# Epsilon as a third triple of the statistics aggregation, a mean scaled in ScalarE's accumulator, and a newly searched instruction order, in a one-core MLP-mixer block

## The chip, the cores and the metric

The kernel runs on one core of one Trainium2 chip. The metric is the device time of one execution in microseconds. Besides the time, every run lists its *span*, from the first to the last instruction of the core.

I use one more length, the *real stretch*: from the start of the first real matmul (tile 1's row matmuls) to the start of the last residual add, both read from the chain of waits. It separates most of the start-up from the rest. One part of the start-up stays inside it: the four row matmuls at its head. They took 1.02 us in most traces, but 1.05 in a_unmean, 1.08 in a_unfold and 1.10 in a_start, where the first of them was slow. Differences of 0.1 us or less are therefore not read as an effect of the change. In the expectations that are quoted below, the same length is given to the modelled end of TensorE's last matmul, which is 0.03 to 0.05 us earlier.

## The reference, cut to what matters

```python
B, S, D, F = 1, 2048, 512, 1792          # bfloat16 throughout

def reference(x, w1, w2, w3, w4):
    h = _gelu(_layernorm(x, axis=-1) @ w1)               # eps 1e-5 in the variance
    # the four quarters of h's channels are shifted by +1, -1, +2, -2 tokens
    hs = jnp.concatenate([g0, g1, g2, g3], axis=-1) @ w2
    x1 = x + hs
    h2 = _gelu(_layernorm(x1, axis=-1) @ w3) @ w4
    return x1 + h2
```

There are 2048 tokens in 16 tiles of 128. Each tile is normalised twice (as x and as x1), so there are 32 statistics; below they are numbered q = 0 to 15 for x and 16 to 31 for x1.

## The kernel before: the parts that matter

The program is a graph of operations. TensorE's order is written down in a script. The other engines' orders come from a list scheduler with priorities, and tables say which engine does what. Everything was tuned by search.

```python
STAT_ACT = (1, 4, 6, 7, 12, 14, 19, ...)     # statistics on ScalarE; the others on VectorE
VPE = {0: "pool", 2: "pool", 4: "pool", ...} # "+ eps" on GpSimd; the others on VectorE
SCRIPT = """
warm:11 ty:1 ty:0 up1:1 ty:2 up1:0 th:1 up1:2 mix:0 ty:3 mix:1 ty:4 up1:3-4 ty:5 mix:2 up1:5 mix:3 ty:16-17
mix:4 up2:0 up1:6 down:0-1 ...
"""
```

Here `warm:11` is 11 matmuls on zeros that are meant to bring the clock up, `ty:n` is the TensorE transpose of a normalised tile n, `up1` and `up2` are the matmuls with w1 and w3, `mix` those with w2 and `down` those with w4. Tile 1 is the first one: its `up1:1` is done in row form, on the rows less their mean, and the standard deviation is put in later by the GELU's scale.

The statistics of one tile, in the two variants:

```python
if q in STAT_ACT:                                    # ScalarE: sum and sum of squares
    act : sum   activation(junk, src, Copy,   accum_out=sums[:, q, 0:1])       # layer 1
    act : ssq   activation(junk, src, Square, accum_out=sums[:, q, 1:2])
    dve : mean  mv[:, q, 0:1] = sums[:, q, 0:1] * (1 / D)
    dve : msq   mv[:, q, 1:2] = mean * mean - eps
    dve : vpe   vpe[q] = ssq / D - msq
else:                                                # VectorE
    dve : bnst  bn_stats(st6[:, q, :], src)          # 6 numbers: two triples
    dve : bnag  bn_aggr(mv[:, q, :], st6[:, q, :])   # mean, variance
    dve or pool : vpe[q] = variance + eps
pool: rstd      rstd[q] = vpe[q] ** -0.5
...             xn = (x - mean) * rstd               # VectorE, ScalarE or GpSimd, by table
```

This is abridged from the kernel's `ln`. The transpose that follows, by TensorE or by DMA, waits for `xn`.

## Time and profile before

| | before |
|---|---|
| time, median of 4 runs | 135.94 us (135.6 to 136.02) |
| span of the profiled run | 134.5 us |
| TensorE busy | 131.4 us, 98% of the span |
| VectorE, ScalarE, GpSimd busy | 54.5, 57.1, 26.9 us |
| first real matmul, real stretch | 6.15 us, 126.50 us |

The engines' busy time, from the page's first part (engine, busy us, share of the span, number of instructions):

```profile
PE 131.4 (98%) x791; PEld 71.8 (53%) x791; DVE 54.5 (41%) x162; ACT 57.1 (42%) x91; POOL 26.9 (20%) x63
```

The chain that ended last, in order of time (start us, us, what):

```profile
0.64 4.51 PE o_ps L700 x11
5.15 0.24 PE y_ps L503 x4
...
5.41 0.61 ACT xnT L511
6.01 0.14 issue
6.15 1.02 PE y_ps L541 x4
...
11.36 0.22 PE y_ps L503 x4
...
132.65 0.29 DVE o_sb L684
```

The chain is TensorE itself but for one piece. L700 are the warm-ups, L503 the transposes, L541 tile 1's row matmuls. Between them TensorE waits while ScalarE evacuates tile 1's transpose (L511, 0.61 us). After 6.15 us no piece of the chain belongs to another engine until the last residual add.

Of the two small instructions that the change removes, the first is this group on the page (source line, engine, operation, shapes, count | busy us, mean ns of one | idle us before it and what ended it). The second, L398, is seen in VectorE's timeline of tile 1's chain (start us, us, what):

```profile
L426 POOL TENSOR_SCALAR vpe<-mv 128x1 f32<-128x1 f32 x10 | 2.3, 233 | 18.0 <-DVE mv L421 17.8
```

```profile
3.32 0.14 DVE L398 TENSOR_SCALAR mv<-sums 128x1 f32<-128x1 f32 x1
3.44 0.18 DVE L421 BATCH_NORM_AGGREGATE mv<-st 128x2 f32<-128x6 f32 x1
3.54 0.32 DVE L454 TENSOR_SCALAR xn_buf<-x_sb,mv 128x512 bf16<-128x512 bf16 x1
```

The separate epsilon is 233 ns on GpSimd (10 tiles) or about 150 ns on VectorE (8 tiles). The separate mean (L398) is 0.14 us. Tile 1's row is ready at 3.54 + 0.32 = 3.86 us, more than 1 us before TensorE takes it.

### The profile page before, as it was taken

To read this page: it belongs to the slowest core of one execution; us is meant where nothing else is said; L and a number is where in the kernel's file an instruction comes from. 1 tells how busy PE (TensorE), PEld (TensorE's weight loads), DVE (VectorE), ACT (ScalarE), POOL (GpSimd) and SP (SyncE) were. 2 spreads that over 40 slices of the span, in tenths; PEclk is the share of its full clock that TensorE was granted. 3 is DMA by queue.
4 is the path that set the end of the run, shared out by engine and by line. 5 is a ranking of instruction groups with operands and counts; after the bars stand their busy time and mean duration, and the time that the engine had idled before them with its cause. 6 is when DMAs were issued, how large, how long until landed. Compare 5 with 4: busy or idle time off the path is not lost.

```text
span 134.5 us, 2035 instructions
## 1 busy us (share of the span) xinstructions
PE 131.4 (98%) x791; PEld 71.8 (53%) x791; DVE 54.5 (41%) x162; ACT 57.1 (42%) x91; POOL 26.9 (20%) x63
## 2 busy tenths in 40 slices
PE   8899999999999999999999999999999999999994
PEld 3388688644566444444444458744444444444463
DVE  2879899689387510171006235052200002232222
ACT  6589625394648866656660003640066530000000
POOL 2645546968044300021002001010000000000000
DMA  6999995644555311003000311103110001111112
GB/s 200 324 385 400 353 255 106 173 81 91 107 120 119 78 39 39 0 0 78 0 0 5 78 39 39 39 0 78 44 39 0 0 0 39 39 44 39 39 42 77
DMA packets 21290, 12.19 MB, mean 91 GB/s; under 512 B 13856, under 2 KB 20768, under 8 KB 21280
## 3 DMA queue, kind: packets, MB, share of 16 engines
q1 hardware_dynamic: 20560, 11.67, 30.9%
q10 hardware_dynamic: 720, 0.39, 1.0%
q8 instruction: 6, 0.10, 0.3%
q14 instruction: 4, 0.03, 0.1%
HBM read 6.82 MB, written 2.10 MB: 66 GB/s over the span
## 4 chain that ended last, share of the span: by engine, by line
PE 98%; ACT 0%; DVE 0%; issue 0%; POOLq 0%
PE y_ps L607 46%; PE o_ps L676 36%; PE o_ps L647 10%; PE o_ps L700 3%; PE y_ps L503 1%; PE y_ps L541 1%; ACT xnT L511 0%; DVE o_sb L684 0%; PE o_ps L578 0%; POOLq L839 0%
## 5 line engine op out<-in xcount | busy, mean ns | idle before, releaser
L607 PE MATMUL y_ps<-xnT,w_sb 128*128 128x512 bf16 (+2 forms) x424 | 63.6, 309 | 0.0
L607 PEld LDWEIGHTS y_ps<-xnT,w_sb 128*128 128x128 bf16 x424 | 38.3, 98 | 24.7 <-DVE xnT L511 0.4
L676 PE MATMUL o_ps<-w_sb,h2T 128*128 128x512 bf16 (+2 forms) x252 | 49.1, 355 | 0.0
L622 ACT ACTIVATE h2T<-y_ps 128x1024 bf16<-128x1024 f32 (+1 forms) x29 | 28.6, 993 | 37.7 <-PE y_ps L607 37.7
L676 PEld LDWEIGHTS o_ps<-w_sb,h2T 128*128 128x128 bf16 x252 | 23.6, 98 | 24.9
L684 DVE TENSOR_TENSOR o_sb<-o_ps,x_sb 128x512 bf16<-128x512 f32 (+2 forms) x18 | 11.3, 630 | 39.9 <-PE o_ps L676 39.9
L437 POOL TENSOR_TENSOR rstd<-vpe,neghalf 128x1 f32<-128x1 f32 x32 | 18.0, 568 | 43.5 <-DVE vpe L405 17.3
L647 PE MATMUL o_ps<-w_sb,hT 128*128 128x512 bf16 x64 | 15.8, 379 | 0.0
L419 DVE BATCH_NORM_STATS2 st<-x_sb 128x6 f32<-128x512 bf16 x18 | 12.2, 688 | 3.4 <-DMA x_sb<-in_x_dram 3.2
L458 DVE TENSOR_SCALAR xn_buf<-x_sb,mv,rstd 128x512 bf16<-128x512 bf16 x20 | 9.5, 476 | 7.3 <-POOL rstd L437 4.1
L658 DVE TENSOR_TENSOR x_sb<-o_ps,x_sb 128x512 bf16<-128x512 f32 x8 | 5.5, 685 | 16.6 <-PE o_ps L647 16.3
L394 ACT ACTIVATE junk<-x_sb 128x512 bf16<-128x512 bf16 x14 | 8.7, 623 | 3.7 <-DVE x_sb L654 3.5
L622 ACT ACTIVATE hT<-y_ps 128x512 bf16<-128x512 f32 (+1 forms) x10 | 8.1, 808 | 3.4 <-PE y_ps L607 3.3
L647 PEld LDWEIGHTS o_ps<-w_sb,hT 128*128 128x128 bf16 x64 | 6.1, 98 | 5.7
L654 DVE SCALAR_TENSOR_TENSOR x_sb<-o_ps,x_sb 128x512 bf16<-128x512 f32 x8 | 5.5, 689 | 7.7 <-PE o_ps L647 7.7
L426 POOL TENSOR_SCALAR vpe<-mv 128x1 f32<-128x1 f32 x10 | 2.3, 233 | 18.0 <-DVE mv L421 17.8
L467 ACT ACTIVATE xn_buf<-x_sb,nmr,rstd 128x512 bf16<-128x512 bf16 x5 | 4.0, 810 | 2.6 <-DVE nmr L463 2.5
L700 PE MATMUL o_ps<-zeros 128*128 128x512 bf16 x11 | 4.5, 595 | 0.6 <-POOLq L839 0.6
L470 POOL TENSOR_SCALAR xn_buf<-x_sb,rstd,nmr 128x512 bf16<-128x512 bf16 x6 | 4.6, 774 | 0.1
L389 ACT ACTIVATE junk<-x_sb 128x512 bf16<-128x512 bf16 x6 | 3.8, 625 | 2.0 <-DMA x_sb<-in_x_dram 2.0
L700 PEld LDWEIGHTS o_ps<-zeros 128*128 128x128 bf16 x11 | 1.5, 143 | 3.1 <-issue 2.5
L421 DVE BATCH_NORM_AGGREGATE mv<-st 128x2 f32<-128x6 f32 x18 | 3.0, 173 | 0.2
(33 smaller groups left out, 30.6 us busy)
## 6 DMA issues: line engine op xcount, KB each, us to landing
out_dram<-o_sb SPq DMA_DIRECT2D x15, 128.0 KB, 1.7
w_sb<-in_w_dram SPq DMA_DIRECT2D x2, 896.0 KB, 9.0
w_sb<-in_w_dram SPq DMA_DIRECT2D x1, 1792.0 KB, 14.2
w_sb<-in_w_dram SPq DMA_DIRECT2D x4, 256.0 KB, 4.8
x_sb<-in_x_dram SPq DMA_DIRECT2D x3, 256.0 KB, 4.6
x_sb<-in_x_dram SPq DMA_DIRECT2D x2, 384.0 KB, 6.1
xnT<-xn_buf SPq DMA_TRANSPOSE x24, 2.5
x_sb<-in_x_dram SPq DMA_DIRECT2D x2, 128.0 KB, 5.9
```

The lines of the kernel that those rows point to most:

```text
L394: (lambda d: (lambda e: e.activation(d, src, ACT_F.Square, accum_out=sums[:, q, 1:2])))(junk[:, b, :]),
L419: pg.add("dve", f"bnst{q}", lambda e: e.bn_stats(st6[:, q, :], src), reads=rs, writes=[(("st6", q), 0)], dur=605)
L437: lambda e: e.tensor_tensor(col(rstd), col(vpe), neghalf[:], ALU.pow),
L458: lambda e: e.tensor_scalar(dst, src, mv[:, q, 0:1], rstd[:, q : q + 1], ALU.subtract, ALU.mult),
L607: ins = e.matmul(y_ps[:, p, W * i : W * (i + 1)], wsb[:, dc, P * fc : P * (fc + 1)], src[:, dc, P * t0 : P * t0 + W], start=(dc == 0), sto ...
L622: (lambda d, s: (lambda e: e.activation(d, s, ACT_F.Gelu_apprx_tanh)))(dst, ysrc),
L647: ins = e.matmul(dst, hT[:, j, c0 : c0 + P], w2_sb[:, j, :], start=(j == 0), stop=(j == DC - 1))
L654: f = lambda e: e.scalar_tensor_tensor(x1_sb[:, t, :], dst, 1.0, x_sb[:, t, :], ALU.mult, ALU.add, accum_out=sums[:, NT + t, 0:1])
L658: f = lambda e: e.tensor_tensor(x1_sb[:, t, :], dst, x_sb[:, t, :], ALU.add)
L676: ins = e.matmul(dst, h2T[:, fc, P * t : P * (t + 1)], w4_sb[:, fc, cs], start=(fc == 0), stop=(fc == FC - 1))
L684: (lambda d, c: (lambda e: e.tensor_tensor(o_sb[:, oi, c], d, x1_sb[:, t, c], ALU.add)))(dst, cs),
L700: ins = e.matmul(o_ps[:, b, :], zeros[:, 0:P], zeros[:], start=True, stop=True)
```

## The change

Its intent has three parts.

1. Epsilon goes into the aggregation. The kernel takes what `bn_stats` leaves as two triples (count, mean, count times variance). A third triple (0, 0, D times eps), written once, is meant to make `bn_aggr` return variance + eps, so that "+ eps" goes away.
2. ScalarE's `Copy` scales by 1/D, so its accumulator is the mean, and the VectorE multiply goes away in layer 1.
3. All tables, the load order and TensorE's script are searched anew, with a refined model of loads and of the cold clock. The hand-found priorities are dropped.

```diff
-        st6 = sb("st6", [P, 2 * NT, 6], F32)
+        st9 = sb("st9", [P, 2 * NT, 9], F32)
+            pg.add("pool", "trip0", lambda e: e.memset(st9[:, :, 6:8], 0.0), ...)
+            pg.add("pool", "trip1", lambda e: e.memset(st9[:, :, 8:9], D * LN_EPS), ...)
 ...
-    e.activation(d, src, ACT_F.Copy, accum_out=sums[:, q, 0:1])
+    e.activation(d, src, ACT_F.Copy, scale=1.0 / D, accum_out=mv[:, q, 0:1])
 ...
-    pg.add("dve", f"bnag{q}", lambda e: e.bn_aggr(mv[:, q, :], st6[:, q, :]), ...)
-    pg.add(VPE.get(q, "dve"), f"vpe{q}",
-           lambda e: e.tensor_scalar(col(vpe), mv[:, q, 1:2], LN_EPS, None, ALU.add), ...)
+    pg.add("dve", f"bnag{q}", lambda e: e.bn_aggr(mv[:, q, :], st9[:, q, :]), ...)
+    var = vpe[:, q : q + 1] if q in STAT_ACT else mv[:, q, 1:2]      # rstd reads it
 ...
-tp16 x0@act x1 w1a w1b x3-4 w2b w2a x5-7 x9-11 w3a w3b x8 w4 tp10 x12-13 x14-15 x2@act
+x0-1 x2 ... w1a ... w1b ... x3 x4-5 w2b w2a ... x7 x8 x6 w3b ... w3a ... x9-10 w4b w4a tp9 x11 x12 x15 x13-14 ...
 ...
-warm:11 ty:1 ty:0 up1:1 ty:2 up1:0 th:1 up1:2 mix:0 ty:3 mix:1 ty:4 up1:3-4 ty:5 mix:2 up1:5 mix:3 ty:16-17 ...
+warm:10 ty:1 ty:0 up1:1 ty:2 up1:0 th:1 up1:2 mix:0 ty:3-4 mix:1 ty:5 up1:3-4 mix:2 ty:16-17 mix:4 up2:0 ...
```

This is cut; the scheduler's model and the other tables (which engine normalises, evacuates, does statistics) change too. TensorE's work stays the same but for one warm-up.

More of the change, by code (lines that the diff above doesn't have):

```diff
@@ L31 @@
     LOOK = {"dve": 300.0, "act": 300.0}
-    DUE = 202650.0
+    DUE = 258005.0
     BEGIN = {"sp": 30.0, "act": 150.0, "pe": 400.0, "dve": 150.0, "pool": 450.0}
     ENTRY = 1900.0
+    COLD, RESTART = 4300.0, 800.0
     LAG = {"load": 150, "tp": 700}
@@ L159, in place @@
         rings = {"sp": [], "act": []}
-        clock = moved = self.total = 0.0
+        fed = {}
+        clock = moved = last = self.total = 0.0
         out = []
@@ L196, in land @@
         def land(op):
-            nonlocal moved
+            nonlocal moved, last
             if op.queue == "tp":
-                at = max(clock + 500.0, op.start + 2450.0) + self.LAG["tp"]
+                at = max(clock + 500.0, op.start + 2450.0, last + 600.0) + self.LAG["tp"]
             elif op.name.startswith("out"):
@@ L204, in land @@
                 moved += op.dur
-                at = clock + 650.0 + min(450.0, 0.25 * moved) + (1200.0 if op.dur > 1400.0 else 0.0) + self.LAG["load"]
+                at = clock + 600.0 + min(600.0, 0.3 * moved) + (600.0 if op.dur > 1400.0 else 0.0) + self.LAG["load"]
+            if op.queue != "tp":
+                last = max(last, at)
+            op.landed = at
             for j in succs[op.idx]:
@@ L230, in place @@
                 tp = op.queue == "tp"
-                free[e] = start + (1300.0 if tp else 460.0)
-                rings[e].append([start + (1400.0 if tp else 1000.0), 600.0 if tp else op.dur, op])
+                free[e] = start + (1300.0 if tp else 500.0)
+                load = op.name.startswith("dma")
+                work = 600.0 if tp else op.dur + (self.RESTART if load and not fed.get(e, True) else 0.0)
+                fed[e] = load
+                rings[e].append([start + (1400.0 if tp else 1000.0), work, op])
                 for j in succs[op.idx]:
@@ L236, in place @@
             else:
-                free[e] = start + op.dur
+                dur = op.dur
+                if e == "pe" and not op.name.startswith("warm"):
+                    dur += min(dur, max(0.0, self.COLD - start))
+                free[e] = start + dur
                 for j in succs[op.idx]:
@@ L240, in place @@
                     hop = self.HOP[e] if o.eng != e else (0.0 if e == "pe" else 120.0)
-                    release(op, o, None if (op.idx, j) in order_only else start + op.dur + hop)
+                    release(op, o, None if (op.idx, j) in order_only else start + dur + hop)
         while (op := finish(1e17)) is not None:
@@ L245, in place @@
         return out
-GROUPS = {1: (1, 1, 1, 1, 1, 1, 2, 4, 2, 2), 2: (2, 4, 4, 4, 2)}
-NORM = {4: "pool", 9: "pool", 11: "pool", 13: "act", 15: "pool", 16: "act", 18: "pool", 20: "pool", 24: "act", 25: "act", 27: "act"}
-EVAC = {2: "dve", 4: "both", 5: "dve", 7: "dve", 8: "dve", 10: "dve", 11: "dve", 16: "dve", 17: "dve", 18: "dve", 19: "dve", 20: "both", 22: "both", 26: "dve", 27: "dve", 28: "both", 29: "both", 31: "dve"}
-SQRT = ()
-STAT_ACT = (1, 4, 6, 7, 12, 14, 19, 21, 23, 24, 25, 27, 29, 31)
@@ L252 @@
-HALF = ()
+GROUPS = {1: (1, 1, 1, 1, 2, 2, 4, 1, 2, 1), 2: (2, 4, 2, 4, 4)}
+NORM = {3: "act", 8: "act", 9: "pool", 10: "pool", 11: "pool", 12: "pool", 14: "act", 15: "pool", 16: "act", 18: "act", 19: "act", 21: "act", 23: "act", 24: "act", 25: "pool", 27: "pool", 28: "act", 29: "pool", 30: "pool", 31: "act"}
+EVAC = {2: "dve", 5: "both", 6: "dve", 8: "dve", 9: "dve", 10: "both", 12: "dve", 14: "dve", 15: "dve", 16: "both", 17: "both", 18: "dve", 19: "both", 21: "dve", 26: "both", 30: "both", 31: "dve"}
@@ L253 @@
+STAT_ACT = (1, 8, 9, 10, 12, 13, 14, 15, 18, 22, 24, 25, 27, 29, 31)
 TAIL = (256, 128, 128)
-VPE = {0: "pool", 2: "pool", 4: "pool", 5: "pool", 6: "pool", 8: "pool", 9: "pool", 14: "pool", 16: "pool", 17: "pool", 19: "pool", 20: "pool", 22: "pool", 24: "pool", 25: "pool", 26: "pool", 31: "pool"}
-NMR = {2: "pool", 3: "pool", 4: "pool", 6: "pool", 7: "pool", 9: "pool", 10: "pool", 11: "pool", 12: "pool", 14: "pool", 18: "pool", 21: "pool", 23: "pool", 25: "pool", 26: "pool", 28: "pool", 29: "pool", 30: "pool", 31: "pool"}
+NMR = {0: "pool", 2: "pool", 3: "pool", 4: "pool", 6: "pool", 7: "pool", 9: "pool", 11: "pool", 12: "pool", 13: "pool", 18: "pool", 19: "pool", 20: "pool", 21: "pool", 22: "pool", 28: "pool", 29: "pool"}
@@ L256 @@
 NAT = (1,)
 SPLIT = ()
-HEV = {1: "dve", 6: "dve"}
-BIAS = {"bnag1": 67, "bnag10": -301, "bnst1": -2084, "bnst10": 1027.66, "bnst14": -605, "bnst15": -1013, "bnst16": -53, "bnst22": -213.193, "bnst7": 1154, "mean1": -1316.81, "mean4": -714.654, "mean5": 1358, "mean8": -649, "msq19": 938, "msq21": -357, "msq3": -971, "msq5": -137.984, "nmr13": -638.801, "nmr15": -1354.5, "nmr16": -514, "nmr19": -721, "norm0": 1112.57, "rstd0": -1069, "rstd10": 709, "rstd16": 1002, "rstd24": 487, "rstd30": -520, "ssq1": -299, "sum12": 418.607, "sum14": 58, "sum15": 149, "sum18": -577, "tp1": -866, "tp19": 1482.81, "tp22": 632.325, "tp3": 119, "tp9": -705.339, "vpe3": 86, "vpe4": -591, "x1_0": 412.151, "x1_11": 1046, "x1_14": -897, "x1_5": 670, "x1_6": 572.538}
+HEV = {1: "dve", 3: "dve"}
@@ L260 @@
+BIAS = {}
 LOADS = """
-tp16 x0@act x1 w1a w1b x3-4 w2b w2a x5-7 x9-11 w3a w3b x8 w4 tp10 x12-13 x14-15 x2@act
+x0-1 x2 tp17 tp16 w1a tp2 w1b tp5 x3 x4-5 w2b w2a tp16 x7 x8 x6 w3b tp1 w3a tp0 x9-10 w4b w4a tp9 x11 x12
+x15 x13-14 tp4
 """
 SCRIPT = """
-warm:11 ty:1 ty:0 up1:1 ty:2 up1:0 th:1 up1:2 mix:0 ty:3 mix:1 ty:4 up1:3-4 ty:5 mix:2 up1:5 mix:3 ty:16-17
-mix:4 up2:0 up1:6 down:0-1 up1:7 mix:5-6 up1:9 mix:9 mix:8 up1:8 mix:7 mix:15 up2:1 mix:14 mix:13 up2:2
-mix:10 down:3-4 down:8 mix:12 up2:4 mix:11 down:2 down:7 down:5 up2:3 down:6 down:10-11 down:9 down:14
@@ L267 @@
-down:12-13 down:15
+warm:10 ty:1 ty:0 up1:1 ty:2 up1:0 th:1 up1:2 mix:0 ty:3-4 mix:1 ty:5 up1:3-4 mix:2 ty:16-17 mix:4 up2:0
+mix:3 up1:5 down:1 down:0 mix:5 up1:6 mix:6 up1:7 mix:9-10 up1:8 mix:7-8 up2:1 mix:12 mix:11 up1:9 mix:13
+up2:2 mix:15 up2:3 mix:14 down:5 down:9 down:2 down:4 up2:4 down:6 down:8 down:3 down:12 down:7 down:10
+down:13 down:11 down:14-15
 """
@@ L303, in bass_standalone__mixer_s_mlp__prompt_kernel @@
         nmr = sb("nmr", [P, 2 * NT], F32)
-        sdv = sb("sdv", [P, 2 * NT], F32)
         sums = sb("sums", [P, 2 * NT, 2], F32)
-        st6b = sb("st6b", [P, len(HALF) + 1, 2, 6], F32)
         hn = sb("hn", [P, len(NAT) + 1, D], BF16)
@@ L343, in consts @@
                    reads=[(("ident",), 0)], writes=[(("ident",), 1)], dur=300)
+            pg.add("pool", "trip0", lambda e: e.memset(st9[:, :, 6:8], 0.0), writes=[(("trip", 0), 0)], dur=90)
+            pg.add("pool", "trip1", lambda e: e.memset(st9[:, :, 8:9], D * LN_EPS), writes=[(("trip", 1), 0)], dur=80)
             pg.add("pool", "epsc", lambda e: e.memset(eps_c[:], LN_EPS), writes=[(("eps",), 0)], dur=70)
@@ L356, in load @@
                 t0, t1 = int(a), int(b or a) + 1
-                if t0 in HALF:
-                    for hh, e2 in ((0, "sp"), (1, "act")):
-                        cs = slice(hh * D // 2, (hh + 1) * D // 2)
-                        yield pg.add(e2, f"dma_x{t0}_{hh}",
-                                     (lambda c: (lambda e: e.dma_start(x_sb[:, t0, c], xt[:, t0, c])))(cs),
-                                     writes=[(("x", t0, hh), 0)], dur=190.0, queue=e2)
-                else:
-                    yield pg.add(eng, f"dma_x{t0}",
-                                 lambda e: e.dma_start(x_sb[:, t0:t1, :], xt[:, t0:t1, :]),
-                                 writes=[(("x", t, hh), 0) for t in range(t0, t1) for hh in (0, 1)],
-                                 dur=(t1 - t0) * 430.0, queue=eng)
+                yield pg.add(eng, f"dma_x{t0}", lambda e: e.dma_start(x_sb[:, t0:t1, :], xt[:, t0:t1, :]),
+                             writes=[(("x", t), 0) for t in range(t0, t1)], dur=(t1 - t0) * 380.0, queue=eng)
             else:
@@ L375, in load @@
                              writes=[((name[:2], c), 0) for c in range(c0, c1)],
-                             dur=(c1 - c0) * P * src.shape[1] * 2 / (300.0 if src.shape[1] == D else 380.0), queue=eng)
+                             dur=(c1 - c0) * P * src.shape[1] * 2 / (345.0 if src.shape[1] == D else 400.0), queue=eng)
                 yield op
@@ L382, in ln @@
             src = x_sb[:, t, :] if layer == 1 else x1_sb[:, t, :]
-            rs = [(("x", t, 0), 0), (("x", t, 1), 0)] if layer == 1 else [(("x1", t), 0)]
+            rs = [(("x", t), 0)] if layer == 1 else [(("x1", t), 0)]
             col = lambda a: a[:, q : q + 1]
@@ L388, in ln @@
                     pg.add("act", f"sum{q}",
-                           (lambda d: (lambda e: e.activation(d, src, ACT_F.Copy, accum_out=sums[:, q, 0:1])))(
-                               junk[:, b, :]),
-                           reads=rs, writes=[(("sum", q), 0), (("junk", b), v)], dur=610)
+                           (lambda d: (lambda e: e.activation(d, src, ACT_F.Copy, scale=1.0 / D,
+                                                              accum_out=mv[:, q, 0:1])))(junk[:, b, :]),
+                           reads=rs, writes=[(("mv", q), 0), (("junk", b), v)], dur=610)
                 b, v = next_junk()
@@ L396, in ln @@
                        reads=rs, writes=[(("ssq", q), 0), (("junk", b), v)], dur=610)
-                pg.add("dve", f"mean{q}",
-                       lambda e: e.tensor_scalar(mv[:, q, 0:1], sums[:, q, 0:1], 1.0 / D, None, ALU.mult),
-                       reads=[(("sum", q), 0)], writes=[(("mv", q), 0)], dur=75)
+                if layer == 2:
+                    pg.add("dve", f"mean{q}",
+                           lambda e: e.tensor_scalar(mv[:, q, 0:1], sums[:, q, 0:1], 1.0 / D, None, ALU.mult),
+                           reads=[(("sum", q), 0)], writes=[(("mv", q), 0)], dur=75)
                 pg.add("dve", f"msq{q}",
@@ L408, in ln @@
             else:
-                if layer == 1 and t in HALF:
-                    k = HALF.index(t)
-                    for hh in (0, 1):
-                        pg.add("dve", f"bnst{q}_{hh}",
-                               (lambda hh: (lambda e: e.bn_stats(st6b[:, k, hh, :],
-                                                                 src[:, hh * D // 2 : (hh + 1) * D // 2])))(hh),
-                               reads=[rs[hh]], writes=[(("st6", q, hh), 0)], dur=335)
-                    pg.add("dve", f"bnag{q}", lambda e: e.bn_aggr(mv[:, q, :], st6b[:, k, :, :]),
-                           reads=[(("st6", q, 0), 0), (("st6", q, 1), 0)], writes=[(("mv", q), 0)], dur=90)
-                else:
-                    pg.add("dve", f"bnst{q}", lambda e: e.bn_stats(st6[:, q, :], src),
-                           reads=rs, writes=[(("st6", q), 0)], dur=605)
-                    pg.add("dve", f"bnag{q}", lambda e: e.bn_aggr(mv[:, q, :], st6[:, q, :]),
-                           reads=[(("st6", q), 0)], writes=[(("mv", q), 0)], dur=75)
@@ L423, in ln @@
-                if q not in SQRT:
-                    eng = VPE.get(q, "dve")
-                    pg.add(eng, f"vpe{q}",
-                           lambda e: e.tensor_scalar(col(vpe), mv[:, q, 1:2], LN_EPS, None, ALU.add),
-                           reads=[(("mv", q), 0)], writes=[(("vpe", q), 0)], dur=70 if eng == "dve" else 240)
-            if q in SQRT:
-                assert q not in STAT_ACT
-                pg.add("act", f"sqrt{q}",
-                       lambda e: e.activation(col(sdv), mv[:, q, 1:2], ACT_F.Sqrt, bias=eps_c[:], scale=1.0),
-                       reads=[(("mv", q), 0), (("eps",), 0), (("warm",), 0)], writes=[(("sdv", q), 0)], dur=190)
-                pg.add("dve", f"rcp{q}", lambda e: e.reciprocal(col(rstd), col(sdv)),
-                       reads=[(("sdv", q), 0)], writes=[(("rstd", q), 0)], dur=75)
-            else:
-                pg.add("pool", f"rstd{q}",
-                       lambda e: e.tensor_tensor(col(rstd), col(vpe), neghalf[:], ALU.pow),
-                       reads=[(("vpe", q), 0), (("neghalf",), 0)], writes=[(("rstd", q), 0)], dur=470)
+                pg.add("dve", f"bnst{q}", lambda e: e.bn_stats(st9[:, q, 0:6], src),
+                       reads=rs, writes=[(("st", q), 0)], dur=605)
@@ new lines, in ln @@
+                pg.add("dve", f"bnag{q}", lambda e: e.bn_aggr(mv[:, q, :], st9[:, q, :]),
+                       reads=[(("st", q), 0), (("trip", 0), 0), (("trip", 1), 0)],
+                       writes=[(("mv", q), 0), (("vpe", q), 0)], dur=75)
+            var = vpe[:, q : q + 1] if q in STAT_ACT else mv[:, q, 1:2]
+            pg.add("pool", f"rstd{q}",
+                   lambda e: e.tensor_tensor(col(rstd), var, neghalf[:], ALU.pow),
+                   reads=[(("vpe", q), 0), (("neghalf",), 0)], writes=[(("rstd", q), 0)], dur=470)
@@ L658, in mm_mix @@
                 f = lambda e: e.tensor_tensor(x1_sb[:, t, :], dst, x_sb[:, t, :], ALU.add)
-            pg.add("dve", f"x1_{t}", f, reads=[(("o", b), v), (("x", t, 0), 0), (("x", t, 1), 0)], writes=wr, dur=600)
+            pg.add("dve", f"x1_{t}", f, reads=[(("o", b), v), (("x", t), 0)], writes=wr, dur=600)
             ln(2, t)
@@ L706, in warm_pe @@
             next_bank()
-        if SQRT:
-            pg.add("act", "warm_sqrt", lambda e: e.activation(warm[:], eps_c[:], ACT_F.Sqrt),
-                   reads=[(("eps",), 0)], writes=[(("warm",), 0)], dur=1400)
         pg.add("act", "warm_gelu", lambda e: e.activation(warm[:], eps_c[:], ACT_F.Gelu_apprx_tanh),
-               reads=[(("eps",), 0)] + [(("sdv", q), 0) for q in SQRT], writes=[(("warm",), 1)], dur=1400)
+               reads=[(("eps",), 0)], writes=[(("warm",), 1)], dur=1400)
         steps = []
```

## The prediction

> **What bounds the kernel now.** TensorE, almost without a gap. The page gives PE 131.4 us busy of a 134.5 us span (98%), granted clock 1.00. The chain of waits is PE for 98% of the span. In time order: 0.64 us to the first warm-up; 11 warm-ups until 5.15; transposes of tiles 1 and 0; a 0.6 us hole in which ScalarE evacuates tile 1's transpose; the first real matmul at 6.15; then PE pieces without a break to 132.63; then 1.9 us of tail (last residual add 0.29, output DMA).
>
> **What the change removes, adds, moves.**
> - Epsilon in the aggregation: 18 "+eps" instructions go (10 on GpSimd at 233 ns, 8 on VectorE at about 150 ns: about 3.5 us of engine time, and one semaphore hop per tile).
> - Mean scaled in ScalarE's accumulator: the VectorE multiply (0.14 us) goes from the first-layer ScalarE tiles. On tile 1, first on PE, that saves about 0.25 us with its hop.
> - Assignment: ScalarE gets 11 normalisations instead of 5 (0.81 us each) and 8 full-statistics tiles instead of 6 (about 1.6 us each), about +8 us; VectorE loses nine normalisations (about 0.45 us each) and the small ops, about -6 us. Estimate: ACT 57 to 65, DVE 54.5 to 49, POOL about 27.
> - PE work: same tile groups by count (five singles, three pairs, one quad, one row tile; two pairs and three quads in layer 2), the same eight PE transposes, one warm-up fewer. Matmuls 791 to 790.
>
> **How much lies on the critical path.** Almost none of the small-op savings. Tile 1's normalised row is finished near 3.9 us, but PE first takes it at 4.98, when the warm-ups end: that chain has 1 us of slack already. What counts is the dropped eleventh warm-up. By the trace warm-ups 1 to 10 start 0.43 us apart, the eleventh 0.32 after the tenth and the first transpose 0.21 after it: the clock came up during the tenth, as the Trainium skill ("TensorE: Matmul & The Clock Gate", Part 1) describes (cold 426.7 ns, warm 215.7 ns at 512 columns, after a window of about 3.4 us). So the eleventh costs only about 0.21 us. Gain: 0.2 us, if w1 (its second half lands near 5.5 us) doesn't get later behind the merged x0-1 load.
> Loads have slack: w3 lands about 14.8 and is first used at 17.4 (new order: needed 0.86 us earlier, with fewer x tiles ahead); w4 about 20.5, used at 25.2.
>
> **Against it.** After 6.15 a new order can only tie or open gaps. Tightest: tile 4's transpose comes about 1 us earlier, tiles 16/17 likewise (tile 17's row was ready 0.1 us before PE took it), and ScalarE, which also does the GELU, gets busier before 30 us. I expect 0 to 0.8 us of new gaps, mean 0.25.
>
> **Prediction.** 135.9 us, 135.3 to 136.9. Faster by over 2%: 0.01; within 2%: 0.95; slower: 0.04.
>
> **What would show each step.** First transpose near 4.77, first real matmul near 5.9; PE gaps after that under 0.8 us in total, all before 30 us; tail unchanged at 1.9 us; no +eps group; aggregation near 0.18 us as before (0.173); rstd waiting on the aggregation itself; ACT busy up by about 8 us.
>
> **What would make it wrong.** The merged x0-1 load or w1 landing over 0.7 us later; the clock coming up later than PE's first real matmuls; a missed transpose DMA after 35 us, which would open a gap of over 1 us.

## The result, and the profile after

| | before | after |
|---|---|---|
| time, median of 4 runs each | 135.94 us | 136.03 us (135.73 to 136.11) |
| ratio after / before | | 1.0007, 95% interval 0.9984 to 1.003 |
| span of the profiled run | 134.5 us | 134.4 us |
| VectorE, ScalarE, GpSimd busy | 54.5, 57.1, 26.9 us | 49.8, 63.9, 27.5 us |
| first real matmul | 6.15 us | 5.88 us |
| real stretch | 126.50 us | 126.66 us |

A ratio is the mean time of one kernel's fast runs over the mean of the other's in the same rounds, so it isn't quite the ratio of the medians. The first real matmul and the real stretch are of the profiled runs.

The busy times after, from the page's first part. Thirteen matmul records are missing from this trace (777 matmuls for 790 weight loads; a group of four shows as three, for instance), so TensorE's busy time isn't comparable to the last digit:

```profile
PE 130.7 (97%) x777; PEld 71.7 (53%) x790; DVE 49.8 (37%) x141; ACT 63.9 (48%) x106; POOL 27.5 (20%) x62
```

The chain after, in order of time:

```profile
0.64 4.25 PE o_ps L680 x10
4.88 0.24 PE y_ps L483 x4
...
5.14 0.61 ACT xnT L491
5.75 0.14 issue
5.88 1.02 PE y_ps L521 x4
...
10.45 0.86 PE o_ps L627 x4
11.31 0.36 PE y_ps L483 x4
...
132.54 0.29 DVE o_sb L664
```

Two things differ. The warm-ups are one fewer, and the first real matmul starts 6.15 - 5.88 = 0.27 us earlier. And at 11.31 the transpose of tile 5 takes 0.36 instead of 0.22 us of the chain: 0.14 us of it is a hole. The rest of the chain is as gapless as before. The sum is -0.27 + 0.14 = -0.13 us, against 132.54 - 132.65 = -0.11 us measured at the chain's end. That is a third of the spread between runs of one kernel (135.6 to 136.02), so the times can't show it.

The hole is explained by VectorE's timeline together with TensorE's:

```profile
10.04 0.69 DVE L638 TENSOR_TENSOR x_sb<-o_ps,x_sb 128x512 bf16<-128x512 f32 x1
10.80 0.41 DVE L438 TENSOR_SCALAR xn_buf<-x_sb,mv,rstd 128x512 bf16<-128x512 bf16 x1
```

```profile
10.29 1.03 PE L627 MATMUL o_ps<-w_sb,hT 128*128 128x512 bf16 x4
11.28 0.40 PE L483 MATMUL y_ps<-ident,xn_buf 128*128 128x128 bf16 x4
```

Tile 5's normalisation (L438) ends at 10.80 + 0.41 = 11.21 us. Its transpose, which TensorE would have reached at about 11.15, starts at 11.28. In the script after, `ty:5` comes right after `mix:1`; before, it came after `ty:4` and two tiles of `up1`. The hop of about 0.07 us from the end of the normalisation to the transpose makes up the rest.

The aggregation that is now also meant to add epsilon, by its source line (durations are min/median/max ns), first before, then after:

```profile
L421 DVE BATCH_NORM_AGGREGATE mv<-st x18: 143/172/183, 3.4 to 81.7; 128x2 f32<-128x6 f32 x18
```

```profile
L412 DVE BATCH_NORM_AGGREGATE mv<-st x17: 151/185/197, 3.6 to 79.5; 128x2 f32<-128x9 f32 x17
```

The third triple costs 13 ns (median 172 to 185), in place of 150 to 233 ns and a hop. All twelve variants below, among them those with the fold, compared correct with the reference. That is no sharp test of epsilon itself: x has a standard deviation of 0.05, a variance of 0.0025, so 1e-5 is 0.4% of it. No run here shows that the third triple is in fact added.

### The profile page after: what moved, and what is told of

Its sections match the earlier page's. It is cut to its first block, busy times and chain, and to the rows that moved or that the text cites. A ratio compares the mean times of both kernels' runs of the same rounds, so it can differ in the third digit from the quotient of the medians.

```text
span 134.4 us, 2025 instructions
## 1 busy us (share of the span) xinstructions
PE 130.7 (97%) x777; PEld 71.7 (53%) x790; DVE 49.8 (37%) x141; ACT 63.9 (48%) x106; POOL 27.5 (20%) x62
## 4 chain that ended last, share of the span: by engine, by line
PE 97%; issue 1%; ACT 0%; DVE 0%; POOLq 0%
PE y_ps L587 46%; PE o_ps L656 36%; PE o_ps L627 10%; PE o_ps L680 3%; PE y_ps L483 1%; PE y_ps L521 1%; ACT xnT L491 0%; DVE o_sb L664 0%; PE o_ps L558 0%; POOLq L816 0%
## 5 line engine op out<-in xcount | busy, mean ns | idle before, releaser
L417 POOL TENSOR_TENSOR rstd<-mv,neghalf 128x1 f32<-128x1 f32 x17 | 9.4, 557 | 29.4 <-DVE mv L412 27.9
L627 PE MATMUL o_ps<-w_sb,hT 128*128 128x512 bf16 x58 | 14.8, 379 | 0.3
L638 DVE TENSOR_TENSOR x_sb<-o_ps,x_sb 128x512 bf16<-128x512 f32 x9 | 6.2, 690 | 19.1 <-PE o_ps L627 19.0
L417 POOL TENSOR_TENSOR rstd<-vpe,neghalf 128x1 f32<-128x1 f32 x15 | 8.3, 557 | 22.3 <-DVE vpe L406 19.2
L394 ACT ACTIVATE junk<-x_sb 128x512 bf16<-128x512 bf16 x15 | 9.3, 623 | 3.3 <-DVE x_sb L634 3.3
L447 ACT ACTIVATE xn_buf<-x_sb,nmr,rstd 128x512 bf16<-128x512 bf16 x11 | 8.8, 810 | 3.6 <-DVE nmr L443 3.0
L450 POOL TENSOR_SCALAR xn_buf<-x_sb,rstd,nmr 128x512 bf16<-128x512 bf16 x9 | 6.9, 767 | 1.5 <-DVE nmr L443 0.8
L438 DVE TENSOR_SCALAR xn_buf<-x_sb,mv,rstd 128x512 bf16<-128x512 bf16 x11 | 5.3, 484 | 2.3 <-POOL rstd L417 1.6
L389 ACT ACTIVATE junk<-x_sb 128x512 bf16<-128x512 bf16 x8 | 5.0, 623 | 1.1 <-DMA x_sb<-in_x_dram 1.1
L443 DVE TENSOR_SCALAR nmr<-mv,rstd 128x1 f32<-128x1 f32 x11 | 2.3, 210 | 4.9 <-POOL rstd L417 4.7
L406 DVE SCALAR_TENSOR_TENSOR vpe<-sums,mv 128x1 f32<-128x1 f32 x15 | 2.8, 189 | 3.3 <-ACT junk L394 3.0
```

Of the source, the lines that this page charges most:

```text
L394: (lambda d: (lambda e: e.activation(d, src, ACT_F.Square, accum_out=sums[:, q, 1:2])))(junk[:, b, :]),
L417: lambda e: e.tensor_tensor(col(rstd), var, neghalf[:], ALU.pow),
L447: f = lambda e: e.activation(dst, src, ACT_F.Identity, bias=nmr[:, q : q + 1], scale=rstd[:, q : q + 1])
L450: f = lambda e: e.tensor_scalar(dst, src, rstd[:, q : q + 1], nmr[:, q : q + 1], ALU.mult, ALU.add)
L627: ins = e.matmul(dst, hT[:, j, c0 : c0 + P], w2_sb[:, j, :], start=(j == 0), stop=(j == DC - 1))
L638: f = lambda e: e.tensor_tensor(x1_sb[:, t, :], dst, x_sb[:, t, :], ALU.add)
```

## The experiments

All were timed in 5 rounds against the kernel before. In the kernels of the table that are marked *held*, each engine's instruction order was pinned to that of the kernel they come from, with only the named operations inserted or deleted. So nothing else was rearranged. The code cuts below are shortened, and some are put in words.

| kernel | first real matmul | real stretch | ratio to before, 95% interval | mean span, its runs / before's of the same rounds |
|---|---|---|---|---|
| before | 6.15 | 126.50 | | |
| after | 5.88 | 126.66 | 1.0007, 0.9984 to 1.003 | |
| b_warm10 | 5.81 | 126.60 | 0.9985, 0.996 to 1.001 | 134.35 / 134.51 |
| a_warm11 | 6.61 | 126.66 | 1.0008, 0.9983 to 1.0033 | 134.73 / 134.51 |
| b_fold (held) | 6.52 | 126.58 | 1.004, 1.0013 to 1.0067 | 134.78 / 134.51 |
| a_unfold (held) | 6.28 | 127.86 | 1.015, 1.012 to 1.018 | 136.43 / 134.51 |
| a_unmean (held) | 6.29 | 126.69 | 1.0024, 1.0 to 1.0049 | 134.62 / 134.64 |
| a_uneps (held) | 6.29 | 127.81 | 1.011, 1.008 to 1.014 | 136.10 / 134.64 |
| b_fold_split (held) | 6.50 | 126.51 | 1.0027, 0.9999 to 1.0056 | 134.72 / 134.64 |
| b_best (held) | 6.08 | 126.52 | 0.9992, 0.997 to 1.0015 | 134.18 / 134.64 |
| b_start (held) | 6.08 | 126.50 | 0.9968, 0.9938 to 0.9997 | 134.30 / 134.77 |
| b_best2 (held) | 5.65 | 127.26 | 0.9975, 0.9945 to 1.0005 | 134.30 / 134.77 |
| a_uneps_dve (held) | 6.29 | 127.05 | 1.0053, 1.0027 to 1.008 | 135.13 / 134.77 |
| a_start (held) | 6.07 | 126.74 | 1.0001, 0.9972 to 1.003 | 134.75 / 134.77 |

The first two columns are of one profiled run each. The mean spans are over 6 runs (this) and 11 (before); the standard deviation of one run's span is 0.1 to 0.5 us. Names that begin with b come from the kernel before, with a from the one after.

My theory at the start (A): TensorE has no gap after its first real matmul, so the only part that can move is the start-up, and the saved small instructions were not on the critical path in the old order. Rivals: the fold did save something and the new order gave it back; or the clock or the loads take back what one warm-up fewer gives.

### One warm-up fewer in the old order, one more in the new

```diff
 # b_warm10, on the kernel before            # a_warm11, on the kernel after, has range(n + 1)
-                for _ in range(n):
+                for _ in range(n - 1):
                     ins = e.matmul(o_ps[:, b, :], zeros[:, 0:P], zeros[:], start=True, stop=True)
```

> The kernel before with one warm-up matmul fewer (10 instead of 11), nothing else. Theory A (only the start-up counts, and the old order has slack elsewhere): first transpose at about 4.72 and first row matmul at about 5.9 instead of 6.15, no new hole after it, so the span falls by 0.2 to 0.27 us against 134.5 and the time by about 0.2 us (ratio near 0.998). Rival R1 (the clock comes up later when PE does less, so the transposes and the row matmuls run slow): first real matmul no earlier than 6.1, ratio 1.000 or above. Rival R2 (the old order also opens a hole when its start is pulled forward): first real matmul at 5.9, and a hole of 0.1 to 0.25 us at the tile 4 or tile 5 transposes.

> The changed kernel with 11 warm-ups again, nothing else. Theory A: first transpose near 4.95, first row matmul near 6.15, the hole of 0.14 us before tile 5's transpose shrinks to between 0 and 0.14 because PE arrives later there; PE work ends near 132.65 to 132.8, time 0 to 0.25 us over the changed kernel (ratio to before 1.000 to 1.002). If the rest of the new order cost anything of its own, it would end later than that: over 0.3 us.

Measured: b_warm10 has its first real matmul at 5.81 us, a real stretch of 126.60 (0.10 more than before: 0.04 at the transpose of tile 1's GELU rows and 0.06 before the first w2 group, not at the transposes of tiles 4 and 5 where R2 had its hole), and a mean span 0.16 us lower. That is a little under the 0.2 to 0.27 of theory A, and the interval of the ratio includes 1, so a gain is not shown by the times. a_warm11 kept its real stretch of 126.66 and its hole, but its first real matmul came at 6.61, later than the 6.15 I had expected. The warm-up groups of these two profiled runs, in TensorE's timeline, say why. First b_warm10, then a_warm11:

```profile
0.64 3.86 PE L700 MATMUL o_ps<-zeros 128*128 128x512 bf16 x10 [0.64 <-POOLq L839]
```

```profile
0.65 4.88 PE L680 MATMUL o_ps<-zeros 128*128 128x512 bf16 x11 [0.65 <-POOLq L816]
```

Ten warm-ups took 4.25 us in the trace after and only 3.86 here; eleven took 4.51 in the trace before and 4.88 here. The clock came up at another moment. In b_warm10 this left the first real matmul waiting for something else. Its transposes began at 4.34 us and tile 1's evacuation ended at 5.36, but the chain of this run starts with w1's second half, which landed at 5.72:

```profile
0.99 4.73 DMA w_sb<-in_w_dram
5.72 0.09 issue
5.81 1.02 PE y_ps L541 x4
```

So 5.81 is near the expected 5.9 by chance: the load set it, and not the missing warm-up. Theory A stands for the real stretch, but its start-up term isn't a constant. It is set by whichever ends last, the evacuation after the clock has come up or w1's second half, and both differ from trace to trace. The earliest clock is in the run a_uneps below, with ten warm-ups in 3.75 us. There too the load came last: w1's second half landed at 6.20 us (1.56 + 4.64), and the first real matmul started at 6.29. In b_best the ten warm-ups took 4.45 us, all slow, and so were the eight transposes after them (1.01 us for the two tiles; 0.61 in the trace before).

```profile
0.64 3.75 PE L682 MATMUL o_ps<-zeros 128*128 128x512 bf16 x10 [0.64 <-POOLq L862]
```

```profile
0.64 4.45 PE L702 MATMUL o_ps<-zeros 128*128 128x512 bf16 x10 [0.64 <-POOLq L884]
4.88 1.01 PE L503 MATMUL y_ps<-ident,xn_buf 128*128 128x128 bf16 x8
```

The Trainium skill ("TensorE: Matmul & The Clock Gate", Part 1) says that the window of the activity monitor runs freely and doesn't reset when the kernel starts, so that the moment varies. These traces agree.

### The new statistics alone, in the old order

```diff
 # b_fold, on the kernel before; every engine's order held
+    trip0, trip1 memsets; bn_aggr over st9; Copy with scale=1/D into mv
-    vpe{q} of the 18 tiles on VectorE statistics, mean{q} of 1, 4, 6, 7, 12, 14
```

> The kernel before with only the new statistics (epsilon as third triple, mean scaled in ScalarE's accumulator); each engine's order is held as it was, the 18 plus-epsilon and 6 mean instructions deleted, two memsets added. Theory A (the saved instructions were never on the critical path): same time, ratio 0.998 to 1.001, PE end 132.6 to 132.7, first real matmul 6.1 to 6.2, while VectorE's busy time falls by about 2 us and GpSimd's by about 2 us. Rival R3 (the fold itself saves 0.3 us or more on the chain, and the new order gave it back): ratio 0.9975 or below.

Measured: the real stretch is 126.58 us against 126.50, although 24 instructions are gone and VectorE's busy time fell from 54.5 to 52.6 and GpSimd's from 26.9 to 24.5. So the part of theory A about the old order holds: there the saved instructions were not on the critical path.

The time was a miss: ratio 1.004, above my range. In the profiled run this is a start-up matter: the first real matmul waited for w1's second half, which landed 5.44 us after its issue (4.54 in the trace before), at 6.43 us by the chain. From its list of waits:

```profile
PE y_ps L541 <- DMA w_sb<-in_w_dram: 0.8, 1, 0.8
```

But that is one run. Over its six runs, half of the excess lies outside the span: time minus span is on average 1.63 us here and 1.33 in the kernel before. The spans alone differ by 134.78 - 134.51 = 0.27 us, with a 95% interval of about 0.36 either way by my reckoning from the runs' scatter. So the excess inside the span isn't resolved.

### The old statistics put back into the new order

```diff
 # a_unfold, on the kernel after; every engine's order held
-    trip0, trip1; bn_aggr over 9 numbers; Copy with scale=1/D into mv
+    mean{q} = sums / D on VectorE just before its first reader
+    vpe{q} = variance + eps, on GpSimd just before rstd{q} or on VectorE just after bnag{q}, by the old table
```

> The changed kernel with the old statistics put back (separate plus-epsilon on the engines that the old table names, separate mean on VectorE), its order on each engine held. Theory A2 (the new order has spent the slack that the fold gave: tile 5's row was already late by 0.14 us): every statistics chain gets 0.15 to 0.35 us longer, the hole before tile 5's transpose grows to 0.3 to 0.5 us, others may open at tiles 16 and 17, so the time rises by 0.2 to 0.6 us over the changed kernel (ratio to before 1.002 to 1.005). Rival (the fold is worth nothing in either order): within 0.1 us of the changed kernel, ratio 1.000 to 1.0015, hole unchanged at 0.14.

Measured: the loss is far larger than expected. The ratio is 1.015, and the real stretch grew from 126.66 to 127.86, by 1.20 us. So theory A as I had it is wrong for the new order: the same instructions that cost nothing in the old order cost over a microsecond there. The next two runs separate the halves.

### Which half: a_unmean and a_uneps

```diff
 # a_unmean: only this of a_unfold            # a_uneps: only this of a_unfold
+    mean{q} = sums / D on VectorE            +    vpe{q} = variance + eps, old table
```

> The changed kernel with only the mean put back as a VectorE multiply (epsilon stays folded), order held. Putting both back cost 1.5% in the time and 1.19 us between the first real matmul and PE's end (127.82 against 126.63). If both halves carry weight, this one gives 0.1 to 0.4 us of that; if epsilon carries all of it (theory), first real matmul to PE end is 126.6 to 126.75 here and the ratio to before is 1.000 to 1.003, the change's own.

> The changed kernel with only epsilon put back as a separate instruction on the engines the old table names (mean stays scaled), order held. Theory: epsilon carries the loss of the earlier run; first real matmul to PE end 127.4 to 127.9 and ratio to before 1.008 to 1.015. Rival (the two halves share it, or it was the added instructions on VectorE): below 127.2 and below 1.007.

Measured: the mean is worth 126.69 - 126.66 = 0.03 us of the real stretch, nothing. Epsilon is worth 127.81 - 126.66 = 1.15 us, nearly all of it, with a ratio of 1.011. a_unmean's ratio of 1.0024 is again from outside its span (1.67 us against 1.32); its mean span equals that of before.

The chain of waits of a_uneps shows the mechanism. It leaves TensorE, which waits in this stretch:

```profile
9.37 0.23 POOL vpe L415
9.60 0.07 issue
9.67 0.58 POOL rstd L419
...
10.35 0.41 DVE xn_buf L440
10.76 0.10 DVE mv L411
10.86 0.08 issue
10.94 0.23 POOL vpe L415
11.17 0.07 issue
11.24 0.58 POOL rstd L419
```

The "+ eps" on GpSimd and its hop, 0.23 + 0.07 us, stand in front of every power. The chain goes aggregation, epsilon, power, normalisation, then on VectorE to the next tile's aggregation, and so on: the delays of tiles 4, 5, 16 and 17 add up in series, because VectorE's next aggregation comes behind the last tile's normalisation in its queue (for tile 16, behind the small `nmr` that prepares it). The chain starts behind VectorE's evacuation of tile 1's transposed GELU, which waits for TensorE itself. That fits a_warm11, where everything came 0.73 us later than in the trace after and the hole stayed as it was.

### Epsilon back, but all of it on VectorE

```diff
 # a_uneps_dve, on a_uneps
-VPE = {0: "pool", 2: "pool", 4: "pool", ...}
+VPE = {}
```

> The changed kernel with epsilon as a separate instruction, all on VectorE (0.15 us each, no extra stop at GpSimd), order held. With the old table (part of them on GpSimd, 0.23 us and a hop) the stretch from first real matmul to PE's end was 127.77 against 126.63. If the price is the longer chain per tile, this one lies between: 126.9 to 127.5. If it is any extra instruction: 127.6 or more. If GpSimd's part alone made it: below 126.8.

Measured: real stretch 127.05 us, 0.39 above the kernel after and between the two as expected; ratio 1.0053. This agrees with a price that goes with the length of the chain per tile. About two thirds of the 1.15 us was the table of engines that a_uneps took over from the old kernel, a table not made for this order. The remaining 0.39 us is what epsilon costs in the new order at its cheapest place among those I tried.

### Is w1's landing what slowed b_fold, and what does the start-up yield?

```diff
 # b_fold_split, on b_fold: tile 1's row matmuls in two operations
-    pg.add("pe", f"rows{t}", part(0, DC), reads=<all four chunks of w1 and of xT>, ...)
+    for hh in (0, 1):
+        pg.add("pe", f"rows{t}_{hh}", part(2 * hh, 2 * hh + 2), reads=<chunks 2*hh, 2*hh + 1>, ...)
 # b_best, on b_fold_split
-    for _ in range(n):                      # warm-ups
+    for _ in range(n - 1):
-EVAC = {2: "dve", ...}
+EVAC = {1: "both", 2: "dve", ...}           # ScalarE and VectorE evacuate half of tile 1 each
```

> The kernel before with the new statistics, as in the earlier run that came out 0.4% slower, and tile 1's row matmuls split in two: the first two wait only for the first half of w1, the last two for its second half. Theory C (that run's loss is only w1's second half landing late, 6.43 against 5.54 us): the first real matmul starts right after the evacuation, 5.75 to 6.15, whatever w1 does unless it lands after about 6.2; ratio falls back to 0.997 to 1.001. Rival (something in the folded statistics itself costs 0.4% in the old order): ratio stays at 1.003 to 1.005.

> As the run before it, with one warm-up fewer (10) and tile 1's transpose evacuated in two halves by ScalarE and VectorE at once: all three start-up terms shortened. If the start-up is all that is left (theory), the first real matmul starts at 5.3 to 5.7 instead of 6.15, the length from there to PE's end stays at 126.5 to 126.6, and the time falls by 0.4 to 0.8 us: ratio 0.994 to 0.997. If w1 or the clock gates it anyway: no earlier than 5.8 and ratio 0.998 or above.

Measured: b_fold_split did not decide it. In its profiled run w1 landed early enough and the clock came up late instead (eleven warm-ups took 4.87 us), so the first real matmul was at 6.50 again. Its ratio of 1.0027 lies between my two ranges, and 0.34 us of it (time minus span 1.66 against 1.32) is outside the span. Its mean span is 0.08 us over that of before: unresolved.

b_best: the three edits bring the mean span down by 134.64 - 134.18 = 0.46 us. My expectation was a miss all the same: it was of the time, 0.4 to 0.8 us, and the time is down by only 0.08%, because this kernel also has 1.68 us outside its span. The ratio and the first real matmul are those of the other case that I had named, a start gated by w1 or the clock. Its first real matmul, at 6.08, was later than the 5.3 to 5.7 expected: this is the run whose warm-ups and transposes were all slow (shown above), and even so it was earlier than before's 6.15.

### The start-up edits alone, in both orders

```diff
 # b_start, on the kernel before: no new statistics; only rows in two halves, EVAC[1] = "both", 10 warm-ups
 # a_start, on the kernel after: rows in two halves, EVAC[1] = "both"
```

> The kernel before with its old statistics and its order held, and three edits at the start-up only: 10 warm-ups, tile 1's row matmuls in two halves that each wait for their half of w1, tile 1's transpose evacuated by ScalarE and VectorE together. Theory (the start-up is the one term left, and it needs no folded statistics): first real matmul between 5.5 and 6.1 as the clock comes up early or late, from there to PE's end 126.4 to 126.6; mean span 0.3 to 0.5 us under that of before in the same rounds, ratio 0.9965 to 0.998. If the old order has no slack without the fold: first real matmul to PE's end 126.7 or more.

> The changed kernel with its order held and the same two start-up edits (row matmuls in two halves, tile 1's transpose evacuated by two engines; it has 10 warm-ups already). First real matmul 0.2 us earlier than its own at the same clock phase (5.5 to 6.1); because its order has a hole at tile 5 already, that hole grows by what the start gains: first real matmul to PE's end 126.75 to 126.95, span within 0.15 us of before's mean, clearly above b_start.

Measured: b_start has a real stretch of 126.50 us, as before, and a mean span 134.77 - 134.30 = 0.47 us lower. Its time is at 0.9968 of before, the whole interval below 1. The old order needs no folded statistics for this. a_start gained nothing measurable: ratio 1.0001, span 134.75 against 134.77. Its real stretch is 126.74; the hole at tile 5 is still there (0.35 us for that transpose) and didn't grow, and the 0.08 us over the trace after are its slow row matmuls (1.10 against 1.02). b_start has the lowest ratio that I have: 135.73 us median against 136.31 of before in the same rounds. Its interval overlaps those of b_warm10 and b_best2, so it isn't shown to be faster than they are; a_start, in the same rounds, has a mean span 0.45 us longer. It is a gain of a third of a per cent, so "same" by the 2% rule. The three edits were not tried one by one in this order. In b_start's profiled run w1's second half landed at 5.34 us, before the evacuation ended, so the split of the row matmuls did nothing there; the evacuation took 0.39 us instead of 0.61.

### Pulling the start further

```diff
 # b_best2, on b_best
-warm-ups 10;  TensorE: tp1 tp0 rows1_0 rows1_1
+warm-ups 9;   TensorE: tp1 rows1_0 tp0 rows1_1
-EVAC = {1: "both", ...}
+EVAC = {0: "both", 1: "both", ...}
```

> Folded statistics in the old order, 9 warm-ups, and the start rearranged: transpose of tile 1, first two row matmuls, transpose of tile 0, last two row matmuls; transposes of tiles 0 and 1 evacuated by two engines. If only the start-up limits, the first real matmul is at 5.1 to 5.6 and PE's end 0.6 to 1.0 us earlier than before. If pulling the start uncovers the next chain (x tiles 2 to 4, whose loads do not move), holes of 0.2 to 0.8 us open before the transposes of tiles 2 to 4, the stretch from first real matmul to PE's end grows to 126.9 to 127.3, and the gain stays at 0.2 to 0.5 us (span).

Measured: the first real matmul was at 5.65, but the real stretch grew to 127.26, by 0.76 us over before. The chain of this run, in order of time:

```profile
5.65 0.78 PE y_ps L541 x2
6.43 0.22 PE y_ps L503 x4
6.65 0.43 PE y_ps L541 x2
7.08 0.22 PE y_ps L503 x4
7.31 0.96 PE y_ps L609 x16
...
8.32 0.40 PE o_ps L580 x4
```

Of the 0.76 us, 0.22 is tile 0's transpose, which now lies inside the stretch (6.43). The first two row matmuls took 0.78 us; two fast ones, with the 0.17 us that the end of a group takes, would be 0.60, so the first was still slow. And the transpose of tile 1's GELU rows (L580) takes 0.40 us where it took 0.22 before: it waited for that GELU, which started at 7.58 us (7.28 in the trace before, although the row matmuls were later there), because ScalarE still had the sum of tile 4 in front of it (6.97 to 7.58, after the later evacuation of tile 0). These three make 0.58 us; the rest is smaller pieces. I had looked for the new holes at tiles 2 to 4; they came at tiles 0 and 1 already. The mean span gain stayed at 134.77 - 134.30 = 0.47 us, no better than b_start.

## Why the prediction was right, and where a step of it was not

**The time: right.** Predicted 135.9 us (135.3 to 136.9), measured 136.03.

**What bounds the kernel: right.** TensorE is gapless after its first real matmul. The real stretch before, 126.50 us, came back as 126.50 to 126.60 in every variant of the old order but b_best2, which put tile 0's transpose inside it, with and without the saved instructions. As it has no holes, I see no order of the same matmuls that would shorten it, and none tried here did.

**The start-up gain: right for the profiled pair, in part by luck, because the term is not a constant.** The prediction had the first transpose near 4.77 and the first real matmul near 5.9, and the profile shows 4.72 and 5.88. It read from one trace that the clock "came up during the tenth" warm-up. The other traces show that it comes up at other moments: ten warm-ups took anything from 3.75 to 4.45 us. In the two traces of the pair it happened to come up at about the same moment, and w1's second half landed before the evacuation ended (5.54 and 5.45 us). The prediction had named this load as its condition; in b_warm10 and b_fold the load came last. By the spacing of fast and slow matmuls, a warm-up fewer should save 0.22 to 0.43 us if nothing else gates the start (an estimate); the mean spans of b_warm10 and before differ by 0.16 us, which isn't resolved.

**New gaps: right.** 0.14 us against an expected 0 to 0.8, before 30 us, the tail unchanged. The place was tile 5, which was not among the tightest that the prediction named.

**The engines' load: right in direction.** ScalarE rose to 63.9 (predicted 65), VectorE fell to 49.8 (49), GpSimd is at 27.5 (27).

**The step that failed: "Almost none of the small-op savings" on the critical path, taken for both orders.** It is true of the old order (b_fold: 126.58 us) and false of the new one. There, putting epsilon back costs 0.39 us at its cheapest place tried and 1.15 us with the old table. The prediction listed the earlier transposes of tiles 4, 16 and 17 as a risk, and didn't see that the shorter chain of the statistics is what keeps that risk down to 0.14 us. The mean's half (0.03 us, all of it in slow row matmuls, 1.05 us against 1.02) is worth nothing in the new order; in the old order both halves together are worth nothing.

So where did the fold's gain go? In the old order it became slack of engines that already had slack. In the new order that slack was spent on earlier transposes, which bought nothing, because TensorE's order was already gapless.

**Open.** Why time minus span is about 1.3 us for some of these kernels (before, after, b_warm10, a_warm11, a_uneps, b_start, a_start), about 1.65 for others (b_fold, a_unmean, b_fold_split, b_best, a_uneps_dve) and about 1.5 for a_unfold and b_best2. It goes neither with the pinned order nor with the third triple: a_start has both and shows 1.32. Whether the fold alone slows the start of the old order, as b_fold's spans hint, is not resolved either. Nor do the traces say why w1's second half took 3.9 to 5.4 us to land in kernels that issue the same loads before it.

## What to carry to other kernels

Where the bounding engine had no gap left, an instruction saved on another engine bought slack and no time here. What it is worth can only be asked together with an order: test it by putting the old instruction back into both orders with everything else pinned. For effects below half a per cent, compare a length inside the profile that leaves out the random start-up, and look at the span and at the time outside it separately before a cause is sought in the kernel's body. What remained to win here was the start-up, 0.47 us of mean span, by three edits together: one warm-up fewer, row matmuls that wait only for their own half of the weights, and one evacuation shared between two engines.

## What the Trainium skill lacked or had wrong

- "TensorE: Matmul & The Clock Gate", Part 1, puts the moment when the clock comes up at about 4 us of sustained activity, give or take 0.5 us; further down, the same part warns that one kernel can have 6, 11 or 14 slow matmuls. The traces show that the first figure is too narrow and side with the warning. In a_uneps, ten warm-ups took 3.75 us, 0.70 less than the 4.45 us of ten slow ones, so the last three were fast already and the clock came up about 3 us after the first warm-up. In b_best, eight transposes that followed without a break took 1.01 us instead of 0.61, so they were all slow, up to about 5.7 us, 5 us after the first warm-up. The page's slow and fast spacing for 512 columns, 426.7 and 215.7 ns, fits: the warm-ups' weight loads start 0.43 us apart, and a group of four mix matmuls takes 0.86 us of the chain.
- "DMA: Bandwidth & Descriptors", Anatomy of one DMA, fits a fixed 2.0 us plus bytes over 436 GB/s, but for DMAs that GpSimd issues; the loads here are issued by SyncE and ScalarE. The first x tile (128 KB) landed 2.3 us after its issue in the trace before, about what the fit would give (an estimate from the page: 2.0 + 0.3). Nothing in that section helps with the fifth transfer issued at the start: w1's second half (256 KB) took 4.54 us in the trace before, 3.9 in b_best and 5.44 in b_fold, with the same transfers ahead of it.
- No page that I found describes the aggregation of batch-norm statistics. The runs show that it takes 172 ns for two triples and 185 for three on 128 partitions (medians).
- No page that I found gives a time for the power on GpSimd: 128x1 took 549 ns (median) in the trace after, and it is the longest of the small instructions in each tile's chain.
